# Causal mask moved from TensorE to GpSimd behind the exp, query padding in front, a rebuilt beginning

## The chip, the cores and the metric

The program runs on one core of a Trainium2 chip. The core has five engines with instruction streams of their own: TensorE (PE in the profile, its weight loads PEld), VectorE (DVE), ScalarE (ACT), GpSimd (POOL) and SyncE (SP), which here issues all DMAs. Each engine works through its stream in order. The metric is the device time of one execution in microseconds; three runs of the kernel before gave 1008.39, 1009.94 and 1011.96, a median of 1009.94.

## The reference

Causal attention with a decay bias over 4 batches, 8 heads, 576 positions and head size 64, then two feed-forward layers of 2304 tokens (512 to 2048 to 512).

```python
def _attn_ref(q, k, v, s):
    scores = scale * np.matmul(q, k.transpose(0, 1, 3, 2))
    causal = np.triu(np.ones((S, S), dtype=bool), k=1)
    cum = np.cumsum(np.maximum(s, 0.0), axis=-1)
    bias = -(cum[:, :, :, None] - cum[:, :, None, :])
    scores = np.where(causal, -1000000000.0, scores + np.minimum(bias, 0.0))
    scores = scores - np.max(scores, axis=-1, keepdims=True)
    attn = np.exp(scores)
    attn = attn / (np.sum(attn, axis=-1, keepdims=True) + 1e-09)
    return np.matmul(attn, v)
# x: heads put side by side, [2304, 512]
h = x @ w_in;  x = (h * np.cos(h)) @ w_out
h = x @ w_in2; y = (np.maximum(h, 0) + np.log1p(np.exp(-np.abs(h)))) @ w_out2
```

## The kernel before

**Attention** (`emit_attention`, u = 0 to 31, one head of one batch each). Two heads share one of three slots in the memory that later holds the late weights (`wlate`). A slot has four tiles: `tbk` and `tbq` (K and Q as high and low parts), `tak` and `taq` (high parts on rows 0 to 63, the decay sums and ones on rows 64 and 65, minus ones and the row maxima on rows 96 to 127). One head goes through these steps:

- The row maxima: six matmuls in four PSUM banks (table `MT`), query block by keys, then one DVE reduction per matmul, which adds `mask` and takes the maximum (line 504). DVE joins the two columns of maxima (line 510), TensorE transposes them, ACT copies them out (line 516), and POOL spreads them with an affine select into rows 96 to 127 of `taq` (line 518, `mq` below).
- The scores, keys by queries, in five tiles (table `STL`): `tbk`·`tbq`, then, in each of the five blocks that lie on the diagonal, a bf16 matmul of `ident` and `tri` that adds -1e30 above the diagonal, then `tak`·`taq`, which brings the main product, the decay and minus the maximum.
- ACT takes the exp of a tile into one of four `pf` buffers (line 558); TensorE multiplies it by V (seven matmuls of fp32, each issued as two), ACT evacuates, a DMA stores the head.

Per pair of heads DVE also forms the low parts (lines 486 and 488), and between heads the first eight weight blocks are converted (lines 421 to 429 and 299, 308).

**The beginning.** POOL fills the constant rows of all three slots, one slot after another, and makes `mask`, `ident` and `tri` by selects. DVE computes the decay sums of all 32 heads, and two DMAs bring those of the first pair to rows 64 and 65 of `tak`. Until there is work, TensorE runs small bf16 matmuls on zeros (`warm`, line 376), as many as the planner put there.

**The feed-forward layers** (`emit_moe`) run over token blocks of 512 (one of 256) and 16 blocks of weights, 24 matmuls each; TensorE is in them from about 211 us on.

**What sets the order.** All operations are put into a `Planner`. Each has a due time built from the table `TUNE` (for a head: `max`, `s`, `av` in units of `ud`), and a cost. The planner simulates the engines, lets each take the ready operation with the earliest due time, and writes the instructions in that order; on the chip each engine then follows it in order and waits on semaphores.

Of the kernel before, what the change touches and what calls it, by code (L numbers as in the profile page):

```python
# [22 lines left out]
QS = (0, 256, 576)  # L23
EARLY, SLOT = 8, 4992
GUARD = True
STG = 1.6
TUNE = dict(lam=61.3799, mu=21.9699, sub1=-0.8, sp4=-0.47, ld4=-2.57, load=-3.32, vload=0.9, split=-0.462, max=-0.4135, s=1.63, av=2.34,
            norm=3.5, md=0.14, sd=0.22, ud=5900.0, e=1.2214, o=2.5648, end=3.5, x0=30.0, xd=2364.0, wa=5.755, wb=4.1769,
            wc=1479.6, wd=9828.5, wg=9000.0, pre=9606.0, we=16928.0, wf=6383.3, backlog=1292.7, hz=16175.7)
# [5 lines left out]
BIG = -3.0e38  # L35
ONE_LO = 1.0 - 2.0 ** -24
# [8 lines left out]
class Planner:  # L45
# [49 lines left out]
    def plan(self, penalty=4000.0):  # L95
# [22 lines left out]
        while left:  # L118
            progress = False
            wake = []  # L120
            for e in free:
# [24 lines left out]
                if e == PE and any(k == ("bank", 7) for k, _ in a[0][3].writes):  # L146
                    self.filler = None
# [19 lines left out]
                _, _, i, o = best  # L167
                _, d, fn = o.opts[i]
# [57 lines left out]
def build(tc, qk, v, s, w1, w2, out):  # L226
# [42 lines left out]
    ident = T("ident", [128, 128], BF16)  # L269
    tri = T("tri", [128, 128], BF16)  # L270
# [8 lines left out]
    sraw, cum = heads[0][0:32], heads[2][0:32]  # L279
# [46 lines left out]
    def fill(vt, ap, val, w, engine=POOL):  # L326
# [3 lines left out]
        P.op(vt, [(POOL, 200.0 + n * 0.83, lambda: G.memset(ap, val)) if engine == POOL else (DVE, 70.0 + n * 0.52, lambda: V.memset(ap, val))], (), w)  # L330
# [4 lines left out]
    V.memset(zero, 0.0)  # L335
    V.memset(mask, 0.0)
    V.memset(ident, 1.0)
    V.memset(tri, 0.0)
# [4 lines left out]
    for i in range(3):  # L343
# [3 lines left out]
        slots.append((tbk, tbq, tak, taq))  # L347
    for i in (2, 0, 1):
        tbk, tbq, tak, taq = slots[i]
        vt = -50000.0 + 1000 * (0 if i == 2 else i + 1)  # L350
        ck = [(("c", i), 0)]
        ag = [((("augk", i), h), "z") for h in range(2)]
        fill(vt, tak.bitcast(F32)[64:96, :, 0:S], 0.0, ag)
        fill(vt + 1, tak.bitcast(F32)[:, :, S:], 0.0, ck)
        fill(vt + 1.5, tak.bitcast(F32)[96:128, :, 0:S], -1.0, [(("cm", i), 0)])
        fill(vt + 2, tbk.bitcast(F32)[:, :, S:], 0.0, [(("cb", i), 0)])
        fill(vt + 2, taq.bitcast(F32)[0:96, :, S:], 0.0, [(("cq", i), 0)])
        fill(vt + 3, taq.bitcast(F32)[64:96, :, 0:S], 0.0, [(("augq", i, h), "z") for h in range(2)])
        P.op(vt + 4, [(POOL, 700.0, lambda taq=taq: G.memset(taq.bitcast(F32)[64:66, :, 0:S], 1.0))], r=[(("augq", i, h), "z") for h in range(2)], w=[(("augq", i, h), 0) for h in range(2)])
        if i == 2:  # L360
            P.op(vt + 8, [(POOL, 660.0, lambda: G.affine_select(out=mask, in_=mask, pattern=[[-1, 640]], compare_op=ALU.is_ge, fill=BIG, base=512, channel_multiplier=1))],
                 (), [("mask", 0)])
            P.op(vt + 9, [(POOL, 250.0, lambda: G.affine_select(out=ident, in_=ident, pattern=[[-1, 128]], compare_op=ALU.is_equal, fill=0.0, base=0, channel_multiplier=1))],
                 (), [("ident", 0)])
            P.op(vt + 10, [(POOL, 250.0, lambda: G.affine_select(out=tri, in_=tri, pattern=[[1, 128]], compare_op=ALU.is_ge, fill=-1.0e30, base=0, channel_multiplier=-1))],  # L365
                 (), [("tri", 0)])
            for x in range(3):
                fill(vt + 10, mr[x].bitcast(F32), 0.0, [(("xl", 1, x), "z")])
            fill(vt + 10.1, eye.bitcast(F32), 1.0, [(("xh", 1, 0), "z")])
            P.op(vt + 10.2, [(POOL, 420.0, lambda: G.affine_select(out=eye, in_=eye, pattern=[[-1, 128]], compare_op=ALU.is_equal, fill=0.0, base=0, channel_multiplier=1))],  # L370
                 [(("xh", 1, 0), "z")], [(("xh", 1, 0), 0)])
        fill(vt + 11, vf[:, (i + 1) % 3, 64], 1.0, [(("vo", (i + 1) % 3), 0)])
# [10 lines left out]
    cumh = [cumt[32 * i:32 * i + 32] for i in range(2)]  # L383
    ckeys = [("tbk", 1), ("tbkl", 1)]
# [6 lines left out]
    P.op(vt + 3, [(DVE, dve_t(S, fast=True), lambda: V.tensor_copy(cumh[0], cum))], r=[(nk[1], "cum")], w=[(ckeys[0], "cum")])  # L391
    P.op(vt + 4, sub_hi(cumh[1], cum, cumh[0], S), r=[(nk[1], "cum"), (ckeys[0], "cum")], w=[(ckeys[1], "cum")])
    for i in range(2):
        dma(-41000.0 + i, cdram[:, i], cumh[i].bitcast(F32), r=[(ckeys[i], "cum")], w=[(("cum", i), 0)])
# [395 lines left out]
```

## Time and profile before

| quantity | value |
|---|---|
| median of three runs | 1009.94 us |
| the profiled execution | 1008.23 us |
| its span, first to last instruction | 1006.4 us |
| PE busy | 998.8 us, 99% |
| DVE, ACT, POOL busy | 690.5, 604.0, 51.2 us |
| granted TensorE clock | 1.0 in every slice |

The span and the busy times are of one execution; what lies around the span is 1.8 us. A busy PE includes overlap of consecutive matmuls, so the distance from one start to the next says what a matmul takes. Of the span, the first 23.4 us are the beginning, up to about 224 us runs attention (with the first feed-forward matmuls among it from 211 us), and the rest is the feed-forward layers.

### The profile page before, as it was taken

How to read it: one execution, taken by the hardware profiler on the slowest of the kernel's cores; microseconds unless marked ns; L12 is line 12 of the kernel's file. 1: busy time of each engine (PE TensorE's matmuls, PEld its weight loads, DVE VectorE, ACT ScalarE, POOL GpSimd, SP SyncE). 2: the span in 40 equal slices, each digit the busy share in tenths (PEclk: the TensorE clock that was granted, in tenths of full speed). 3: DMA queues.
4: the chain of work that ended last, by engine and by line, in shares of the span. 5: the costliest groups of instructions: out<-in, count | busy, mean ns of one | idle time of the engine just before them, and what ended most of it. 6: DMA issues, size and time to landing. Idle time of an engine off the chain costs nothing.

```text
span 1006.4 us, 14198 instructions
## 1 busy us (share of the span) xinstructions
PE 998.8 (99%) x5180; PEld 842.3 (84%) x5180; DVE 690.5 (69%) x1284; ACT 604.0 (60%) x1062; POOL 51.2 (5%) x68
## 2 busy tenths in 40 slices
PE   9999999999999999999999999999999999999998
PEld 7888888878888889988888888888888998888886
DVE  8889888879964536445357989995565756555553
ACT  5777777777655445555456668665454655445444
POOL 8111112100000000000000000000000000000000
PEclk9999999999999999999999999999999999999999
DMA  6676666663422212002012335221130201001001
GB/s 209 212 209 188 194 189 185 190 211 113 155 84 91 90 51 101 26 22 64 1 65 99 135 130 189 88 80 49 35 115 1 84 1 42 1 1 42 1 1 42
DMA packets 40488, 95.29 MB, mean 95 GB/s; under 512 B 7074, under 2 KB 13730, under 8 KB 36322
## 3 DMA queue, kind: packets, MB, share of 16 engines
q1 hardware_dynamic: 40418, 94.39, 29.5%
q8 instruction: 40, 0.66, 0.3%
q14 instruction: 30, 0.25, 0.1%
HBM read 66.87 MB, written 18.64 MB: 85 GB/s over the span
## 4 chain that ended last, share of the span: by engine, by line
PE 93%; DVE 2%; DMA 2%; POOL 1%; issue 1%; ACT 0%; SPq 0%; DVEq 0%; POOLq 0%; ACTq 0%
PE bank L322 93%; PE bank L376 1%; DMA stage<-w 1%; DVE bc L504 1%; DMA adram<-num 0%; POOL wlate L330 0%; DMA raw<-rdram 0%; DMA raw<-adram 0%; DVE wlate L488 0%; DVE wlate L486 0%; DVE conv L429 0%; DMA rd<-adram 0%; DVE xl L308 0%; DVE raw L614 0%; POOL tri L365 0%
## 5 line engine op out<-in xcount | busy, mean ns | idle before, releaser
L322 PE MATMUL bank<-xh,wearly 128*128 128x512 f32 (+1 forms) x640 | 193.8, 369 | 1.2 <-DVE pf L658 1.2
L322 PE MATMUL bank<-xh,wlate 128*128 128x512 f32 (+1 forms) x640 | 193.7, 368 | 0.0
L322 PE MATMUL bank<-ghi,wlate 128*128 128x512 f32 (+1 forms) x640 | 193.5, 368 | 0.0
L322 PE MATMUL bank<-ghi,wearly 128*128 128x512 f32 (+1 forms) x640 | 193.5, 368 | 0.0
L299 ACT ACTIVATE ghi<-pf 128x512 fp32r<-128x512 f32 (+1 forms) x160 | 93.8, 587 | 141.9 <-DVE pf L670 92.0
L308 DVE TENSOR_TENSOR glo<-pf,ghi 128x512 fp32r<-128x512 f32 (+1 forms) x160 | 102.0, 637 | 77.4 <-ACT ghi L299 76.9
L322 PE MATMUL bank<-wlate 128*128 128x320 f32 (+9 forms) x576 | 150.5, 363 | 1.3 <-POOL xl L330 1.2
L322 PEld LDWEIGHTS bank<-xh,wearly 128*128 128x128 f32 x640 | 117.3, 189 | 21.7 <-DVE pf L658 1.6
L322 PEld LDWEIGHTS bank<-ghi,wlate 128*128 128x128 f32 x640 | 117.3, 189 | 20.0
L322 PEld LDWEIGHTS bank<-xh,wlate 128*128 128x128 f32 x640 | 117.3, 189 | 19.9
L322 PEld LDWEIGHTS bank<-ghi,wearly 128*128 128x128 f32 x640 | 117.3, 189 | 19.8
L322 PE MATMUL bank<-pf,vf 128*65 128x320 f32 (+4 forms) x448 | 127.9, 384 | 0.0
L322 PE MATMUL bank<-xl,wearly 128*128 128x512 f32 (+1 forms) x320 | 117.9, 369 | 0.0
L322 PE MATMUL bank<-glo,wlate 128*128 128x512 f32 (+1 forms) x320 | 117.9, 368 | 0.0
L322 PE MATMUL bank<-xl,wlate 128*128 128x512 f32 (+1 forms) x320 | 117.8, 368 | 0.0
L322 PE MATMUL bank<-glo,wearly 128*128 128x512 f32 (+1 forms) x320 | 117.8, 368 | 0.0
L322 PEld LDWEIGHTS bank<-wlate 128*128 128x128 f32 (+1 forms) x576 | 95.5, 191 | 17.7 <-POOL xl L330 1.4
L666 DVE SCALAR_TENSOR_TENSOR bc<-pf 128x512 f32<-128x512 f32 (+1 forms) x80 | 51.0, 637 | 81.7 <-ACT pf L664 81.7
L504 DVE CUSTOM_DVE_ANT_0 bc<-bank,mask 128x384 bf16<-128x384 f32 (+3 forms) x192 | 82.0, 468 | 15.7 <-PE bank L322 10.8
L558 ACT ACTIVATE pf<-bank 128x256 f32<-128x256 f32 (+2 forms) x160 | 66.7, 433 | 38.1 <-PE bank L322 33.3
L654 DVE SCALAR_TENSOR_TENSOR pf<-pf,pf 128x512 f32<-128x512 f32 (+1 forms) x80 | 50.7, 635 | 56.3 <-ACT pf L652 56.3
L663 ACT ACTIVATE pf<-bank 128x512 f32<-128x512 f32 (+1 forms) x80 | 44.3, 554 | 68.4 <-PE bank L322 65.7
(75 smaller groups left out, 1331.5 us busy)
## 6 DMA issues: line engine op xcount, KB each, us to landing
stage<-w SPq DMA_DIRECT2D x32, 1024.0 KB
raw<-qk SPq DMA_DIRECT2D x15, 576.0 KB
wlate<-wlate SPq DMA_DIRECT2D x30, 288.0 KB
vf<-v SPq DMA_DIRECT2D x32, 160.0 KB
adram<-num SPq DMA_DIRECT2D x32, 146.2 KB
xdram<-num SPq DMA_DIRECT2D x18, 256.0 KB
out<-num SPq DMA_DIRECT2D x18, 256.0 KB
raw<-adram SPq DMA_DIRECT2D x32, 128.0 KB
```

Of the source, the lines that this page charges most:

```text
L299: opts.append((ACT, act_t(n, psum), (lambda: A.activation(o, i, AF.Copy, scale=1.0 if scale is None else scale))))
L308: return [(DVE, dve_t(n), lambda: V.tensor_tensor(o, a, hi.bitcast(F32), op=ALU.subtract))]
L322: X.matmul(o, a, b, start=st, stop=sp, skip_group_check=skip)
L376: X.matmul(bank[7][:, 0:256], zero[:, 0:128], zero, start=True, stop=True)
L504: P.op(tx + 1, [(DVE, dve_t(w, True) + DX, lambda bk=bk, off=off, w=w, mo=mo, col=col, pr=pr, jk=junk[i if x < 2 else x - 2]: V.tensor_ten ...
L558: P.op(tx + 3, [(ACT, act_t(wt, True) + AX, lambda pt=pt, bk=bk, wt=wt: A.activation(pt[:, :wt], bank[bk][:, :wt], AF.Exp))], r=[(("bank", ...
L654: P.op(te + 2, [(DVE, dve_t(n), lambda a0=a0, a1=a1: V.scalar_tensor_tensor(a1, a1, MAGIC, a0, op0=ALU.subtract, op1=ALU.subtract))], r=[( ...
L663: P.op(te, [(ACT, act_t(n, True), lambda a0=a0, hp=hp: A.activation(a0, hp, AF.Abs))], r=hr, w=[(k0, (tg, "a"))])
L666: P.op(te + 2, [(DVE, dve_t(n), lambda a0=a0, a2=a2: V.scalar_tensor_tensor(a2, a0, 2.0, a0, op0=ALU.subtract, op1=ALU.mult, reverse0=True))],
```

## The change

- **Mask.** The matmuls of `ident` and `tri` go. Behind the exp, a POOL affine select per diagonal block writes zeros above the diagonal of `pf` in place (new line 571), and the matmul with V waits for the last select of its tile. Rows 66 to 95 of `tak` and `taq` (all 0 before) get a staircase in steps of 20 positions, whose product is a very negative score, made by selects from the small tile `cst` (lines 357, 370).
- **Padding.** 64 columns of zeros stand in front of the queries in `taq` (`QP`) and no longer behind, so the query blocks of the maxima end at 64, 192, 320, 448 and 576 instead of 128, 256, 384, 512 and 576. `MT` is cut anew.
- **Beginning.** DVE writes the decay rows of the first pair straight into `tak` (new line 396, `s` comes with the first two heads' rows repeated on other partitions); the fills of POOL wait until the first of them is done (`quiet`), those of slots 0 and 1 for the spread of the maxima of heads 0 and 1 (`later`). The low parts of the first pair are formed in halves. The first weight block and two V tiles are loaded earlier.
- **Order.** `TUNE` and a few costs have other numbers.

```diff
+QP = 640 - S
...
+    quiet = [("cumdone", 0)]
+    P.op(-95000.0, [(POOL, 150.0, lambda: G.affine_select(out=cst[:, 2:4], ...
+        later = ([(("mq", 2, 0), 0)], [(("mq", 2, 1), 1)], [])[i]
+        P.op(vt if later else -94000.0, [(POOL, 1300.0, lambda taq=taq: G.affine_select(out=taq[64:96, :, QP:], in_=cst[64:96, 1:2].unsqueeze(2).broadcast_to((32, 2, S)), pattern=[[0, 2], [1, S]],
+                                                                     compare_op=ALU.is_ge, fill=FAR, base=STEP, channel_multiplier=-STEP))], later, [(("augq", i, h), 0) for h in range(2)])
...
+        fill(vu + 1, tak.bitcast(F32)[:, :, S:], 0.0, [(("c", i), 0)], r=later or quiet)
...
-    P.op(vt + 4, sub_hi(cumh[1], cum, cumh[0], S), r=[(nk[1], "cum"), (ckeys[0], "cum")], w=[(ckeys[1], "cum")])
+    for x in range(2):
+        y = slice(32 + 32 * x, 34 + 32 * x)
+        P.op((vt + 4, -1000.0)[x], [(DVE, dve_t(S), lambda x=x, y=y: V.scalar_tensor_tensor(slots[2][2][64:66, x, 0:S], cumt.bitcast(F32)[y], cst[y, 2 + x:3 + x], cum[y], op0=ALU.mult, op1=ALU.add))],
+             r=[(nk[1], "cum"), (ckeys[0], "cum"), ("cst", 0)], w=[((("augk", 2), x), 0)] + ([("cumdone", 0)] if x == 0 else []))
...
-    MT = [[(4, 0, 320, 4, 0), (0, 0, 128, 0, 320)], [(1, 0, 256, 1, 0), (4, 320, 256, 9, 256)], [(2, 0, 384, 2, 0)], [(3, 0, 512, 3, 0)]]
+    MT = [[(4, 0, 320, 4, 0), (1, 0, 192, 1, 320)], [(3, 0, 448, 3, 0), (0, 0, 64, 0, 448)], [(2, 0, 320, 2, 0)], [(4, 320, 256, 9, 0)]]
...
-                    dma(t + 20 + x, tak.bitcast(F32)[64:66, x, 0:S], cumt.bitcast(F32)[x:x + 33:32], r=[(i, "cum") for i in ckeys], w=[((kaugk, x), 0)])
...
-                if x != 1:
-                    ml.append((o[:, 0:min(w, 128)], ident, tri[:, :min(w, 128)], False, False, True, 0))
-                ml.append((o, tak[:, sl, ks], taq[:, sl, qs:qs + w], False, True, True, w))
+                ml.append((o, tak[:, sl, ks], taq[:, sl, QP + qs:QP + qs + w], False, True, True, w))
...
+            done = bt
+            for i, (j, qs, off, w) in enumerate(lst):
+                if qs == 128 * j:
+                    dw = min(w, 128)
+                    P.op(tx + 4 + i, [(POOL, 220.0 + 1.4 * dw, lambda z=pt[:, off:off + dw], dw=dw: G.affine_select(
+                        out=z, in_=z, pattern=[[1, dw]], compare_op=ALU.is_ge, fill=0.0, base=0, channel_multiplier=-1))],
+                        r=[(("pf", pi), done)], w=[(("pf", pi), (bt, i))])
+                    done = (bt, i)
```

In TensorE's stream, in the middle of attention, a stretch of the kernel before reads as follows (`wlate` is score and maximum matmuls, `pf,vf` the matmuls with V, each of which is two instructions).

```order
L322 MATMUL bank_68<-wlate 128x320
L322 LDWEIGHTS ident
L322 MATMUL bank_68<-tri,ident 128x128
L322 MATMUL bank_70<-pf_95,vf 65x320
L322 MATMUL bank_68<-wlate 128x320
L322 MATMUL bank_69<-wlate 128x192
L322 LDWEIGHTS ident
L322 MATMUL bank_69<-tri,ident 128x128
```

A stretch of the changed kernel at the same stage:

```order
L323 MATMUL bank_70<-pf_96,vf 65x64
L323 MATMUL bank_72<-pf_94,vf 65x320
L323 MATMUL bank_68<-wlate 128x320 x2
L323 MATMUL bank_66<-wlate 128x256 x2
L323 MATMUL bank_69<-wlate 128x192 x2
L323 MATMUL bank_69<-wlate 128x64 x2
L323 MATMUL bank_71<-pf_95,vf 65x128
```

The two score matmuls of a block now stand side by side, and no mask stands among them.

POOL's stream at the beginning, before (`xl` are the maxima's scratch tiles, L518 the first two spreads of maxima):

```order
L363 AFFINE_SELECT ident<-ident 128x128
L365 AFFINE_SELECT tri<-tri 128x128
L330 MEMSET xl_84 128x128 x3
L330 MEMSET xh_82 128x128
L370 AFFINE_SELECT xh_82<-xh_82 128x128
L330 MEMSET vf 128x5
L330 MEMSET wlate 32x2x576
L330 MEMSET wlate 128x2x64
...
L359 MEMSET wlate 2x2x576
L330 MEMSET vf 128x5
L518 AFFINE_SELECT wlate<-xl_84 32x640
L518 AFFINE_SELECT wlate<-xh_82 32x640
```

And in the changed kernel (L357 and L370 make the staircase rows, L527 is the spread of maxima, L571 the new mask):

```order
L357 AFFINE_SELECT wlate<-cst 32x2x576
L370 AFFINE_SELECT wlate<-cst 32x2x576
L363 AFFINE_SELECT mask<-mask 128x640
L331 MEMSET wlate 128x2x64 x2
...
L370 AFFINE_SELECT wlate<-cst 32x2x576
L527 AFFINE_SELECT wlate<-xl_84 32x640
L357 AFFINE_SELECT wlate<-cst 32x2x576
L331 MEMSET wlate 96x2x64
L571 AFFINE_SELECT pf_94<-pf_94 128x128
L527 AFFINE_SELECT wlate<-xh_82 32x640
```

The first spread stands ahead of the fills of two slots instead of behind them, and from there on masks and spreads share one queue.

DVE's stream from the decay sums to the first reductions (L504, L513), before:

```order
L391 CAST wlate<-num 32x576
L308 TENSOR_TENSOR wlate<-num,wlate 32x576
L486 TENSOR_TENSOR wlate<-raw_85,wlate 64x2x576
L488 SCALAR_TENSOR_TENSOR wlate<-raw_85,wlate 64x1152
L504 ISA bc,mx<-bank_66,mask 128x256
```

And in the changed kernel:

```order
L393 CAST wlate<-num 96x576
L396 SCALAR_TENSOR_TENSOR wlate<-wlate,cst,num 2x576
L309 TENSOR_TENSOR wlate<-num,wlate 32x576
L396 SCALAR_TENSOR_TENSOR wlate<-wlate,cst,num 2x576
L513 ISA bc,mx<-bank_65,mask 128x320
```

The low parts of the first pair moved from ahead of the first reductions to behind them, in halves of 576 columns, and two small operations joined the chain.

## Rows read from the trace of the kernel before

**Rows 1.** The page, busy time, share and instructions of each engine.

```profile
PE 998.8 (99%) x5180; PEld 842.3 (84%) x5180; DVE 690.5 (69%) x1284; ACT 604.0 (60%) x1062; POOL 51.2 (5%) x68
```

**Rows 2.** Stretches: length, PE, PEld, DVE, ACT, POOL busy (count), clock, DMA share, GB/s.

```profile
0.00:23.41 23.41, 20.95 (x158) 17.04 (x158) 20.66 (x55) 12.13 (x15) 21.51 (x38) 1.00 0.63 194
23.41:224.50 201.09, 199.73 (x1232) 165.33 (x1230) 174.72 (x483) 149.28 (x310) 29.65 (x31) 1.00 0.67 198
224.50:1002.60 778.10, 778.08 (x3792) 659.97 (x3792) 495.16 (x747) 441.98 (x737) 0.00 (x0) 1.00 0.19 64
```

**Rows 3.** The chain that ended last, first 60 us: shares by engine and line.

```profile
by line: PE bank L322 69.0%; PE bank L376 15.1%; POOL wlate L330 6.6%; issue 2.4%; POOL tri L365 2.3%; POOL mask L361 1.4%; POOL ident L363 1.3%; POOL xl L330 0.7%; POOL wlate L359 0.2%; POOLq L361 0.1%; POOLq L365 0.0%; POOLq L783 0.0%
```

**Rows 4.** Timeline of PE around 134 us: start, us, what.

```profile
132.92 0.23 PE L322 MATMUL bank<-tri,ident 128*128 128x128 bf16 x1
132.99 0.74 PE L322 MATMUL bank<-pf,vf 128*65 128x320 f32 x2
133.33 0.64 PE L322 MATMUL bank<-wlate 128*128 128x320 f32 x2
...
134.29 0.20 PE L322 MATMUL bank<-tri,ident 128*128 128x64 bf16 x1
134.33 0.77 PE L322 MATMUL bank<-pf,vf 128*65 128x320 f32 x2
134.70 0.55 PE L322 MATMUL bank<-wlate 66*128 66x320 f32 x1
```

**Rows 5.** Timeline of PE at 184 us, with no mask in front.

```profile
184.18 0.71 PE L322 MATMUL bank<-pf,vf 128*65 128x320 f32 x2
184.48 0.52 PE L322 MATMUL bank<-wlate 66*128 66x256 f32 x1
```

**Rows 6.** Groups by form on PE, the mask: busy us, mean ns.

```profile
L322 PE MATMUL bank<-tri,ident 128*128 128x128 bf16 x128 | 29.3, 230 | 0.0
L322 PE MATMUL bank<-tri,ident 128*128 128x64 bf16 x32 | 6.6, 206 | 0.0
```

**Rows 7.** Groups by form on DVE, widest and narrowest reduction of the maxima.

```profile
L504 DVE CUSTOM_DVE_ANT_0 bc<-bank,mask 128x512 bf16<-128x512 f32 x32 | 21.8, 681 | 0.5
L504 DVE CUSTOM_DVE_ANT_0 bc<-bank,mask 128x128 bf16<-128x128 f32 x32 | 8.9, 277 | 0.0
```

**Rows 8.** Timeline of PE in the beginning, the warm-up matmuls (the second row is part of the first).

```profile
1.18 7.16 PE L376 MATMUL bank<-num 128*128 128x256 bf16 x43 [1.18 <-DVE num L335]
...
5.64 2.71 PE L376 MATMUL bank<-num 128*128 128x256 bf16 x22
9.51 1.15 PE L322 MATMUL bank<-wlate 66*128 66x320 f32 x6 [1.16 <-POOL xl L330]
```

**Rows 9.** Timeline of DVE in the beginning.

```profile
2.76 0.78 DVE L388 TENSOR_SCALAR num<-num 32x576 f32<-32x576 f32 x1 [1.07 <-DMA num<-s]
...
4.95 1.41 DVE L391 CAST wlate<-num 32x576 fp32r<-32x576 f32 x1
...
7.57 1.35 DVE L486 TENSOR_TENSOR wlate<-raw,wlate 64x1152 fp32r<-64x1152 f32 x1
...
10.34 0.42 DVE L504 CUSTOM_DVE_ANT_0 bc<-bank,mask 128x256 bf16<-128x256 f32 x1
...
21.46 1.64 DVE L486 TENSOR_TENSOR wlate<-raw,wlate 64x1152 fp32r<-64x1152 f32 x1
```

**Rows 10.** Timeline of POOL, the first two spreads of maxima.

```profile
21.15 0.75 POOL L518 TENSOR_SCALAR_AFFINE_SELECT wlate<-xl 32x640 fp32r<-32x640 f32 x1
21.85 1.86 POOL L518 TENSOR_SCALAR_AFFINE_SELECT wlate<-xh 32x640 fp32r<-32x640 f32 x1
```

**Rows 11.** Groups by form on ACT and POOL: busy us, mean ns.

```profile
L558 ACT ACTIVATE pf<-bank 128x320 f32<-128x320 f32 x64 | 27.8, 434 | 11.0 <-PE bank L322 10.2
...
L518 POOL TENSOR_SCALAR_AFFINE_SELECT wlate<-xl 32x640 fp32r<-32x640 f32 x16 | 16.2, 1012 | 84.6 <-ACT xl L516 84.5
...
L330 POOL MEMSET xl<- 128x128 f32 x3 | 0.5, 205 | 0.0
```

More of the change, by code (lines that the diff above doesn't have):

```diff
@@ L35 @@
 BIG = -3.0e38
+STEP, FAR = 20, -1.2676506002282294e30
 ONE_LO = 1.0 - 2.0 ** -24
@@ L167, in plan @@
                 _, _, i, o = best
+                if e == PE and any(k == ("bank", 7) for k, _ in o.writes):
+                    self.filler = None
                 _, d, fn = o.opts[i]
@@ L324, in mms, with fill @@
         return [(PE, d, go)]
-    def fill(vt, ap, val, w, engine=POOL):
+    def fill(vt, ap, val, w, engine=POOL, r=()):
         n = 1
@@ L329, in fill @@
             n *= x
-        P.op(vt, [(POOL, 200.0 + n * 0.83, lambda: G.memset(ap, val)) if engine == POOL else (DVE, 70.0 + n * 0.52, lambda: V.memset(ap, val))], (), w)
+        P.op(vt, [(POOL, 80.0 + n * 0.88, lambda: G.memset(ap, val)) if engine == POOL else (DVE, 70.0 + n * 0.52, lambda: V.memset(ap, val))], r, w)
     for i in range(2):
@@ L347, in build @@
         slots.append((tbk, tbq, tak, taq))
+    quiet = [("cumdone", 0)]
+    P.op(-95000.0, [(POOL, 150.0, lambda: G.affine_select(out=cst[:, 2:4], in_=cst[:, 2:4], pattern=[[32, 2]], compare_op=ALU.is_ge, fill=-1.0, base=32, channel_multiplier=-1))], (), [("cst", 0)])
     for i in (2, 0, 1):
         tbk, tbq, tak, taq = slots[i]
[L350 to L359, printed above, removed]
@@ L360, in build @@
-        if i == 2:
[L361 to L366, printed above, removed]
+        vt = (700.0, 20000.0, -50000.0)[i]
@@ new lines, in build @@
+        fill(vt + 0.1 if later else -93000.0, taq.bitcast(F32)[0:96, :, 0:QP], 0.0, [(("cq", i), 0)], POOL if later else DVE, later)
+        fill(vu + 1, tak.bitcast(F32)[:, :, S:], 0.0, [(("c", i), 0)], r=later or quiet)
+        fill(vu + 2, tbk.bitcast(F32)[:, :, S:], 0.0, [(("cb", i), 0)], r=later or quiet)
+        if i == 2:
+            P.op(-50001.0, [(POOL, 760.0, lambda: G.affine_select(out=mask, in_=mask, pattern=[[-1, 640]], compare_op=ALU.is_ge, fill=BIG, base=512, channel_multiplier=1))],
+                 quiet, [("mask", 0)])
@@ L371, in build @@
+            P.op(vt + 3.2, [(POOL, 380.0, lambda: G.affine_select(out=eye, in_=eye, pattern=[[-1, 128]], compare_op=ALU.is_equal, fill=0.0, base=0, channel_multiplier=1))],
                  [(("xh", 1, 0), "z")], [(("xh", 1, 0), 0)])
-        fill(vt + 11, vf[:, (i + 1) % 3, 64], 1.0, [(("vo", (i + 1) % 3), 0)])
+        P.op((-40000.0, 19900.0, -91000.0)[i], [(POOL, 1300.0, lambda tak=tak: G.affine_select(out=tak[64:96, :, 0:S], in_=cst[64:96, 0:1].unsqueeze(2).broadcast_to((32, 2, S)), pattern=[[0, 2], [1, S]],
+                                                                     compare_op=ALU.is_ge, fill=0.0, base=STEP, channel_multiplier=-STEP))], (quiet, later, [])[i], [((("augk", i), h), "z") for h in range(2)])
@@ L382, in build @@
     cumt = slots[1][0].rearrange("p h n -> p (h n)")[:, 0:S]
-    cumh = [cumt[32 * i:32 * i + 32] for i in range(2)]
-    ckeys = [("tbk", 1), ("tbkl", 1)]
+    cuml = slots[1][1].rearrange("p h n -> p (h n)")[:, 0:S]
+    cumh = [cumt[0:32], cuml[0:32]]
+    ckeys = [("tbk", 1), (("tbql", 1), 0)]
     vt = -60000.0
```

75 lines of the change are left out of this document (40 added, 35 removed).

## The prediction

> **What bounds the kernel now.** I read the page's busy times first, then the stretches, then the chain of waits at the beginning, then TensorE's timeline in the middle of attention, and last the groups by form of the operations that the change touches. TensorE is busy 998.8 of 1006.4 us [rows 1], and the stretches show where it is not: it loses most before 23.4 us; from there to 224.5 us it is busy 199.7 of 201.1 us, and in the feed-forward layers 778.1 of 778.1 [rows 2]. So an instruction less on TensorE shortens the run by what it occupies, as long as no other engine comes up beside it. The nearest is VectorE, busy 174.7 us in the attention stretch, 87% [rows 2]; GpSimd has 29.7 us of work there. In the beginning the chain runs over the warm-up matmuls (line 376): 15.1% of the first 60 us, 9.0 us, all behind the first real matmul at 9.51 us [rows 3, 8]. These only pass the time; they and what lies ahead of 9.51 us are lost time, some 19 us in all.
>
> **The mask matmuls.** 128 of 128 columns and 32 of 64 go [rows 6]. Their mean times of 230 and 206 ns contain the overlap, so I take starts. A mask of 128 starts at 132.92 and the next matmul at 132.99: 0.07 us; a 128-column stream of 0.44 ns a column (below) is 0.06, so I take 0.065. The matmul with V behind it then takes 0.34 us to the next other start (132.99 to 133.33) [rows 4], the same one behind a long matmul 0.30 (184.18 to 184.48) [rows 5]: the load of V has only the short mask to hide under, and 0.04 us of it show. That is 0.105 us each, 13.4 us for 128. A mask of 64 occupies 0.04 us (134.29 to 134.33), and the V matmul behind it 0.37 (134.33 to 134.70) [rows 4]; but what it will follow instead is a 64-column score matmul, just as short, so the 0.07 stay and I count 32 x 0.04 = 1.3 us. Sum 14.7 us. Bounds: 9.6 if the exposed load shows again somewhere else in all cases (128 x 0.065 + 1.3), 17.6 if all 160 give 0.11.
>
> **The padding.** The six maximum matmuls of a head have 1856 columns now (320, 128, 256, 256, 384, 512) and 1600 afterwards (320, 192, 448, 64, 320, 256). The feed-forward stretch has 3840 matmuls less a few that run earlier, with 1.77 million columns, in 778.1 us [rows 2]: 0.44 ns a column. 256 columns are 0.113 us, 3.6 us for 32 heads. Against it the narrowest is now 64 instead of 128 wide and hides 0.03 us less of the load behind it (0.07 against 0.04 above): 1.0 us. I take 2.6 us, bounds 1.6 and 3.6. VectorE gains too: between 512 and 128 columns its reduction goes from 681 to 277 ns [rows 7], 1.05 ns a column, so 0.27 us a head, 8.6 us of its 174.7.
>
> **The beginning.** The first real matmul starts at 9.51 us, behind 43 warm-up matmuls, of which 21 had started before 5.64 us [rows 8], and behind the decay rows, which a DMA brings after the operation that follows the cast. The changed order has 24 warm-ups first, done by about 6 us, and no DMA: the sums arrive at 2.76 us, maximum and scan end at 4.95 [rows 9], the cast takes 1.41 us beside a running fill and perhaps 0.5 without one (GpSimd's fills now wait), and the new operation of 576 columns about 0.7, half of the 1.35 us of a 1152-column one [rows 9]. That is 6.2 to 7.1 us; the transfer of `s` is three times as large and may add 0.3. I take 6.5 us, 3.0 us earlier. After it the changed order has 71 warm-ups where 81 stood, at 0.111 us (9.0 us by 81) 1.1 us less. Against the sum of 4.1 us stands VectorE: it did the low parts of the first pair (from 7.57 us) while it had nothing else, before the first reduction at 10.34 [rows 9]; now these 2.7 us come between the reductions of heads 0 and 1, and two new operations stand in front. The first spread of maxima, at 21.15 us [rows 10] behind the fills of two slots, can start soon after its maxima are there, some 6 us earlier; but heads 2 and 3 are paced by VectorE, which is no further by then. I take 3.0 us in all, bounds a loss of 1 (VectorE gives all of it back) and a gain of 5.
>
> **What is added.** 160 selects on GpSimd, between exp and the matmul with V. No row has one in this place. For its price the bounds are 0.205 us, a fill of the same 128x128 that reads nothing, and 0.75 us, the undisturbed select of 640 columns [rows 10, 11]; with a fifth of the columns it is nearest to the fill, and I take 0.25. That is 40 us of GpSimd's time in the stretch on top of 29.7, so GpSimd does not become full. Whether TensorE waits is a matter of distance. Priced by the rows above, the matmuls between the last score matmul of a tile and its first V matmul were worth at least 0.7 us and in the middle 1.5 to 2.1 (by kind of tile), and with an exp of 0.43 us [rows 11] and its handovers that was enough, since TensorE hardly waited [rows 2]. In the changed order they are worth at least 1.2 and in the middle 2.2 to 3.6 us. The select and one handover more, about 0.5 us, thus fit in the added distance. What can break it is a select that is held up. The spread at 21.85 us took 1.86 us instead of 0.75, beside a subtraction that took 1.64 instead of 1.35 [rows 9, 10], and the mean of these selects is 1.01 [rows 11]. A hold of about 1 us on a part of the tiles is more than the shortest distances bear. Queued behind a held select are the other masks and the spread of the next head's maxima, for which its score matmuls wait. Bounds: 0 if the distance bears all, 42 us if TensorE waits the mean excess of 0.26 us (1.01 less 0.75) on each of 160 tiles. I take 3 us: 0.26 us on about 12 of the 160, since half of the tiles have a distance of more than twice what they need.
>
> The held spread bears on a rule of the Trainium skill, page "SBUF — State Buffer", section "Who interferes with whom": a GpSimd instruction that reads SBUF and a VectorE instruction with two SBUF inputs (or in a two-port mode) shut each other out for the whole instruction, while one that only writes is free of the two-input kind. The subtraction and the spread above agree with it. By that rule the fill is too cheap a neighbour for the new selects, and the change puts 160 readers beside an engine that is 87% busy; taken to its end this is the first rival below.
>
> Sum against the profiled execution: 1008.23 - 14.7 - 2.6 - 3.0 + 3 = 990.9 us. That execution is 1.7 us below the median of the runs shown, so for a median I forecast 992 us. The other renumbered due times move feed-forward work only within a stretch where TensorE has no gap, and I cost them at nothing; what hides them is that VectorE and ScalarE have 495 and 442 us of work in 778 [rows 2]. Were that cover gone, TensorE would wait at the change of stage, and I would double the 1.4 us that it is idle in the whole attention stretch [rows 2].
>
> **The rivals.**
> - VectorE becomes the bound of attention. For: 87% busy, and selects and its two-input operations shut each other out. Its work falls to 174.7 - 8.6 = 166.1 us, while TensorE's falls to 199.7 - 17.3 = 182.4. If each select takes its 0.205 us from VectorE, that is 166.1 + 32.8 = 198.9, and the stretch stays where it is: only the beginning's 3 us and 0.8 us are left, 1006 us. Against: where a hold shows in the rows, it is beside a subtraction of a pair, of which attention has 32, and not beside the 192 reductions.
> - TensorE waits for held masks, and it becomes slower. Place: the matmul with V of the diagonal tiles, behind the select in GpSimd's queue. The gain without waits is 20.3 us, and it decides from 0.127 us a tile, half of the mean excess of 0.26 us. At three quarters (31 us) the time is 1021 us. For: a mean of 1.01 us against 0.75, and four `pf` buffers, which now stay taken for longer. Against: the distance in the order has grown by more than an undisturbed select needs.
> - No waits, and the beginning gives its 5 us: 1009.94 - 17.3 - 5 = 987.6, or 985 with the higher bound for the masks.
>
> **How the numbers follow.** Forecast 0.74, with its own range of 985 to 999 from the bounds of masks and beginning and up to 9 us of waits; the case without waits 0.07; VectorE as the bound 0.10; held masks 0.09. A measurement of this kernel can tell about 0.3%, 3 us, from no change. Faster: 0.74 + 0.07 and half of the 0.10, 0.86; within 0.3% the other half, 0.05; slower 0.09. The range of 983 to 1004 leaves out 0.19 above (and next to nothing below).
>
> **What would show it.** In the profile of the changed kernel: attention's PE busy time near 182 us with the first feed-forward matmuls about 17 us earlier; the first real matmul near 6.5 us; the first spread near 15 us; 128x128 selects near 0.25 us in the middle and some over 1 us beside subtractions; idle time of PE in front of V matmuls of about 3 us. The forecast is wrong if VectorE is over 95% busy between 25 and 200 us, or if PE's idle time there is over 10 us and is put down to POOL, or if the matmuls with V stay at 0.34 us without the masks.

## The result and the profile after

| | before | after |
|---|---|---|
| median of the runs | 1010.45 us (1008.39 to 1011.96) | 997.36 us (995.03 to 1000.12) |
| ratio | | 0.9873, interval 0.9841 to 0.9905 |
| the profiled execution | 1008.23 us | 998.2 us |

The changed kernel is 12.8 us (3.2 either way) faster; the forecast was 992, with a range of 983 to 1004. The time is within the range and 5 us above the forecast. Below, the difference of two kernels is the difference of their ratios to the kernel before, times 1010 us, since each was timed beside its own runs of it.

The page's busy times of the changed kernel, which answer to [rows 1]:

```profile
PE 982.8 (99%) x4991; PEld 835.1 (84%) x4991; DVE 684.2 (69%) x1289; ACT 605.6 (61%) x1063; POOL 124.2 (12%) x223
```

The stretches of the changed kernel (length, then busy time of PE, PEld, DVE, ACT and POOL with counts, granted clock, DMA share, GB/s), against [rows 2]:

```profile
0.00:24.00 24.00, 20.58 (x139) 16.50 (x140) 20.52 (x60) 13.07 (x19) 15.64 (x33) 1.00 0.64 210
24.00:208.00 184.00, 179.61 (x1045) 155.87 (x1044) 164.54 (x477) 143.61 (x302) 108.57 (x191) 1.00 0.72 207
208.00:992.00 784.00, 782.04 (x3810) 662.65 (x3809) 499.14 (x754) 447.85 (x743) 0.00 (x0) 1.00 0.20 65
```

PE lost 16.0 us of busy time, but its idle time grew. It is 4.4 us between 24 and 208 us now, and 2.0 us behind 208 us, at the change of stage. In [rows 2] the attention stretch of before has 1.4 us, but 1.2 of these are its own wait at the change of stage, which the cut at 224.50 us puts into that stretch. Up to 205 us it was idle for only 0.2 us (a stretch and PE's timeline of the kernel before):

```profile
23.41:205.00 181.59, 181.40 (x1138) 150.48 (x1137) 158.16 (x461) 134.59 (x284) 29.65 (x31) 1.00 0.67 196
```

```profile
224.52 0.50 PE L322 MATMUL bank<-xh,wearly 128*128 128x512 f32 x1 [1.19 <-DVE pf L658]
```

GpSimd works 109 us in attention instead of 30, and VectorE is still at 89%.

The beginning of VectorE, timeline of the changed kernel (start, us, engine, line, operation), against [rows 9]:

```profile
3.71 0.46 DVE L390 TENSOR_SCALAR num<-num 96x576 f32<-96x576 f32 x1 [1.84 <-DMA num<-s]
4.20 1.75 DVE L391 TENSOR_TENSOR_SCAN num<-num 96x576 f32<-96x576 f32 x1
5.99 0.46 DVE L393 CAST wlate<-num 96x576 fp32r<-96x576 f32 x1
6.56 0.81 DVE L396 SCALAR_TENSOR_TENSOR wlate<-wlate,cst,num 2x576 fp32r<-2x576 f32 x1
...
9.80 0.49 DVE L513 CUSTOM_DVE_ANT_0 bc<-bank,mask 128x320 bf16<-128x320 f32 x1
```

And of TensorE, its first real matmul, against [rows 8]:

```profile
7.52 0.98 PE L323 MATMUL bank<-wlate 66*128 66x320 f32 x6 [1.21 <-ACT wlate L476]
```

The sums arrive at 3.71 us, 0.95 later than before. The first matmul is 2.0 us earlier, the first reduction only 0.54. The view names ScalarE's copy of line 476, which ended at 7.52 us, as what released the matmul; the decay rows ended at 7.37 (6.56 and 0.81), so which of the two held it isn't settled.

TensorE in the middle of attention, timeline of the changed kernel, against [rows 4, 5]:

```profile
135.15 0.65 PE L323 MATMUL bank<-wlate 128*128 128x320 f32 x2
135.63 0.70 PE L323 MATMUL bank<-pf,vf 128*65 128x320 f32 x2
135.93 0.89 PE L323 MATMUL bank<-wlate 128*128 128x256 f32 x5
...
148.19 0.28 PE L323 MATMUL bank<-wlate 128*128 128x64 f32 x1
148.30 0.79 PE L323 MATMUL bank<-pf,vf 128*65 128x320 f32 x2
148.68 0.84 PE L323 MATMUL bank<-wlate 128*128 128x320 f32 x3
```

Behind a long score matmul the matmul with V takes 0.30 us (135.63 to 135.93), behind one of 64 columns 0.38, as it did behind a mask.

The selects: groups by form on POOL (busy us, mean ns), and who waits for them between 24 and 208 us (us in all, times, longest):

```profile
L571 POOL TENSOR_SCALAR_AFFINE_SELECT pf<-pf 128x128 f32<-128x128 f32 x128 | 61.5, 486 | 47.0 <-ACT pf L565 45.1
L571 POOL TENSOR_SCALAR_AFFINE_SELECT pf<-pf 128x64 f32<-128x64 f32 x32 | 12.6, 395 | 0.1
```

```profile
PEld bank L323 <- POOL pf L571: 4.2, 8, 0.9
PE bank L323 <- POOL pf L571: 1.9, 5, 0.6
```

The median of all 160 is 292 ns, the longest 1504. Of the 45 that took over 0.45 us, 41 ran beside a VectorE operation with two operands in SBUF, of the 111 under 0.31 us 36. TensorE's weight load waits eight times for a select, and its matmul five times.

The change of stage, PE's timeline of the changed kernel:

```profile
213.36 0.39 PE L323 MATMUL bank<-ghi,wearly 128*128 128x512 f32 x1
215.70 0.50 PE L323 MATMUL bank<-glo,wearly 128*128 128x512 f32 x1 [1.96 <-DVE glo L309]
```

VectorE stood 2.03 us in its queue before a multiply whose operand a DMA brought (line 629, at 214.24 us), with the operation that TensorE needed behind it.

### The profile page after: what moved, and what is told of

The parts are those of the page before. It is cut to its first block, busy times and chain, and to the rows that moved or that the text cites. A ratio compares the mean times of both kernels' runs of the same rounds, so it can differ in the third digit from the quotient of the medians.

```text
span 996.2 us, 14023 instructions
## 1 busy us (share of the span) xinstructions
PE 982.8 (99%) x4991; PEld 835.1 (84%) x4991; DVE 684.2 (69%) x1289; ACT 605.6 (61%) x1063; POOL 124.2 (12%) x223
## 4 chain that ended last, share of the span: by engine, by line
PE 90%; DVE 3%; DMA 2%; ACT 1%; POOL 1%; issue 1%; SPq 0%; DVEq 0%; POOLq 0%; ACTq 0%
PE bank L323 90%; DMA wlate<-wlate 1%; POOL pf L571 1%; DVE bc L513 1%; DMA raw<-adram 1%; ACT pf L565 1%; DMA raw<-rdram 0%; DVE wlate L495 0%; DVE raw L629 0%; DVE wlate L497 0%; DMA num<-s 0%; POOL wlate L527 0%; ACT wlate L482 0%; DVE wlate L396 0%; DMA adram<-num 0%
## 5 line engine op out<-in xcount | busy, mean ns | idle before, releaser
L323 PE MATMUL bank<-xh,wlate 128*128 128x512 f32 (+1 forms) x640 | 206.6, 368 | 0.0
L323 PE MATMUL bank<-ghi,wlate 128*128 128x512 f32 (+1 forms) x640 | 205.9, 368 | 0.0
L323 PE MATMUL bank<-ghi,wearly 128*128 128x512 f32 (+1 forms) x640 | 205.2, 368 | 0.0
L323 PE MATMUL bank<-xh,wearly 128*128 128x512 f32 (+1 forms) x640 | 205.1, 369 | 0.0
L323 PE MATMUL bank<-wlate 128*128 128x320 f32 (+9 forms) x576 | 134.4, 344 | 4.2 <-DMA wlate<-wlate 1.8
L323 PE MATMUL bank<-pf,vf 128*65 128x320 f32 (+4 forms) x448 | 125.5, 383 | 2.0 <-POOL pf L571 1.9
L323 PEld LDWEIGHTS bank<-wlate 128*128 128x128 f32 (+1 forms) x576 | 93.0, 190 | 20.1 <-DVE conv L430 1.6
L513 DVE CUSTOM_DVE_ANT_0 bc<-bank,mask 128x320 bf16<-128x320 f32 (+3 forms) x192 | 75.6, 430 | 7.8 <-PE bank L323 4.0
```

The source lines that it names most:

```text
L513: P.op(tx + 1, [(DVE, dve_t(w, True) + DX, lambda bk=bk, off=off, w=w, mo=mo, col=col, pr=pr, jk=junk[i if x < 2 else x - 2]: V.tensor_ten ...
```

## The experiments

**No selects.** The order is the changed kernel's, the place of the selects in it too.

```diff
-    P.op(tx + 4 + i, [(POOL, 220.0 + 1.4 * dw, lambda ...: G.affine_select(out=z, ...))],
+    P.op(tx + 4 + i, [(POOL, 220.0 + 1.4 * dw, lambda: None)],
```

> The changed kernel with the 160 mask selects planned but not issued, so every other engine keeps its order; the block above the diagonal is masked only by the staircase of 20 positions. It gives what the selects cost in waits and in disturbance of VectorE. Theory A (waits behind the selects ate the shortfall of 5 us against the forecast): 5 to 8 us faster than the changed kernel, about 990 to 992. Rival B (the selects are hidden, the beginning or transfers ate it): within 2 us of the changed kernel, about 996.

Measured: 994.61 us, ratio 0.9845 (0.9824 to 0.9866), 2.8 us below the changed kernel, between the two expectations; the two intervals overlap. In the two profiles the same matmuls stand in the same order, and up to 205 us the distances from start to start are in sum 5.3 us longer with selects. This profile also showed a thing that varies from run to run. Its timeline of PE at the change of stage, and stretches around it:

```profile
211.35 0.80 PE L323 MATMUL bank<-glo,wearly 128*128 128x512 f32 x1 [2.88 <-DVE glo L309]
```

```profile
205.00:210.00 5.00, 3.48 (x16) 2.55 (x14) 1.68 (x4) 2.52 (x4) 0.00 (x0) 1.00 0.79 242
210.00:215.00 5.00, 3.65 (x9) 2.88 (x10) 5.00 (x10) 3.04 (x5) 0.00 (x0) 0.55 0.24 50
215.00:220.00 5.00, 5.00 (x19) 4.04 (x18) 5.00 (x6) 3.80 (x6) 0.00 (x0) 0.77 0.47 107
```

TensorE was idle for 2.88 us, and then had a granted clock of 0.55, near its lower level of 1.2 GHz. The lead of 5.3 us over the changed kernel's profile was 1.9 at the end of the span (994.3 against 996.2); the longer wait makes 0.9 of the difference, and the fall of the clock, by what is left, about 2.5. In the changed kernel no fall followed the wait of 1.96 us.

**The kernel before without its mask matmuls.** The order is that of before; the decay is clipped on the other side, so that exp sees no large numbers.

```diff
-            for o, a, b, st, sp, skip, _ in lst:
+            for o, a, b, st, sp, skip, n in lst:
+                if n == 0:
+                    continue
-    V.tensor_scalar_max(sraw, sraw, 0.0)
+    V.tensor_scalar_min(sraw, sraw, 0.0)
```

> The kernel before with its 160 mask matmuls planned but not issued, order kept; the mask is left out, and the decay is clipped to its negative part (minimum for maximum) so that the exps stay finite. It gives the gross price of the mask on TensorE. The forecast's row price (0.105 us for 128, 0.04 for 64 columns): 14.7 us faster than before, about 995.5. Rival (only their streams count, the exposed load shows again elsewhere): 9.6 us, about 1001.

Measured: 1005.41 us, ratio 0.9955 (0.9939 to 0.9971): 4.5 us, a third of what I had priced. The profile is of an execution of 1009.08 us, 3.7 above the median, so it shows more loss than the median has. Its stretch of attention, and waits there (us in all, times, longest):

```profile
23.41:224.50 201.09, 195.80 (x1083) 166.02 (x1081) 175.69 (x485) 149.65 (x313) 32.48 (x31) 0.98 0.68 200
```

```profile
DVE bc L506 <- PE bank L324: 8.6, 8, 1.8
PEld bank L324 <- DVE xl L512: 6.7, 12, 2.3
...
PEld bank L324 <- DVE mx L506: 5.0, 13, 0.7
...
DVE rd L587 <- DMA rd<-adram: 4.2, 2, 2.7
...
PE bank L324 <- DVE xl L512: 3.2, 7, 1.8
...
PE bank L324 <- DVE mx L506: 0.9, 3, 0.3
```

Instruction by instruction against the kernel before, the distances across the missing masks are 7.6 us shorter up to 205 us, and the other distances 6.9 us longer. Of the 6.9 us, 4.5 lie between 127 and 137 us, at one wait and what followed it (below). TensorE waits for VectorE's maxima (lines 506, 512), 25 times in its weight loads and ten times, 4.1 us, in its matmuls, and VectorE for TensorE's banks. I read this as two engines that keep an order made for matmuls that are no longer there; the trace doesn't show that reason by itself. The largest single wait, on VectorE and then on PE:

```profile
127.70 0.18 DVE L587 TENSOR_SCALAR rd<-rd 128x18 f32<-128x18 f32 x1 [2.72 <-DMA rd<-adram]
...
128.77 0.17 DVE L512 TENSOR_TENSOR xl<-mx 128x5 fp32r<-128x5 f32 x1
```

```profile
128.99 0.48 PE L324 MATMUL bank<-xh,xl 128*128 128x128 f32 x1 [1.82 <-DVE xl L512]
```

A small step of the normalization (line 587) waits for its transfer and holds the reductions behind it. In the next stretch the granted clock was 0.50, which is the level of 1.2 GHz:

```profile
130.00:135.00 5.00, 5.00 (x19) 4.02 (x18) 4.06 (x14) 2.67 (x6) 0.65 (x1) 0.50 0.38 91
```

**The mask back on TensorE, everything else as changed, order planned anew.**

```diff
+                if x != 1:
+                    ml.append((o[:, 0:min(w, 128)], ident, tri[:, :min(w, 128)], False, False, True, 0))
...
-                if qs == 128 * j:
+                if False:
```

> The changed kernel with the mask back on TensorE (identity and triangle matmuls, planned anew) and no selects; padding, beginning and due times stay. It gives what moving the mask is worth net of waits. If the move is most of the change (forecast 14.7 less 3): 10 to 12 us slower than the changed kernel, about 1008. Rival (the due times of the new order alone gave most): within 5 us of the changed kernel.

Measured: 1013.53 us, ratio 1.0023 (1.0003 to 1.0043): 15.2 us above the changed kernel and even slower than before. TensorE was idle for 6.0 us between 24 and 208 us of its profile, and between 215 and 240 us the clock was 0.86, so its size isn't the masks' alone. It also shows that the new numbers, the padding and the beginning don't make the kernel faster by themselves while the planner has masks to place. That led to a repeat in a fixed order (below).

**No V loads behind the third head** (V of other heads is used).

```diff
-        dma(at(st["vload"]) ..., vl[:, 0:64], v[u], ...)
+        dma(at(st["vload"]) ..., vl[:, 0:64], v[u], ..., skip=u > 2)
```

> The changed kernel without the V loads of heads 3 to 31 (those heads use old V tiles), order kept: 4.6 MB less in the attention stage, about 14% of its traffic. Rival C (transfers limit the attention stage, whose DMA share is 0.72 to 0.76): 4 us or more faster. Theory A (only waits behind selects matter): within 2 us of the changed kernel.

Measured: 994.78 us, ratio 0.9854 (0.9835 to 0.9872), 1.9 us below the changed kernel, with intervals that overlap. The share of the transfers in the time is small, and not settled by this run.

**The padding alone, in the kernel before.**

```diff
+QP = 640 - S
-    MT = [[(4, 0, 320, 4, 0), (0, 0, 128, 0, 320)], [(1, 0, 256, 1, 0), (4, 320, 256, 9, 256)], [(2, 0, 384, 2, 0)], [(3, 0, 512, 3, 0)]]
+    MT = [[(4, 0, 320, 4, 0), (1, 0, 192, 1, 320)], [(3, 0, 448, 3, 0), (0, 0, 64, 0, 448)], [(2, 0, 320, 2, 0)], [(4, 320, 256, 9, 0)]]
```

> The kernel before with the padding and the new cut of the maximum matmuls alone, planned anew with its own due times. The forecast's term (TensorE columns): 2.6 us faster than before, about 1007. Rival D (padding helps through VectorE's shorter reductions only where VectorE holds TensorE up, which it did not do before): within 1 us of the term, not more than 4 us either.

Measured: 1007.74 us, ratio 0.9977 (0.9968 to 0.9987): 2.3 us less, 1.3 to 3.2.

**The same, with the mask matmuls not issued and the decay clipped** (both edits above).

> The same with the mask matmuls planned but not issued (mask left out, decay clipped to its negative part), order kept. Theory D (without the masks VectorE's reductions held TensorE up, as the wait for them of 9.4 us in the trace without masks says, and the padding takes 0.27 us a head off them): 5 us or more below the pad-only kernel, 999 to 1002. Rival (the masks are worth only 4.4 us in any order): 1003.

Measured: 1005.72 us, ratio 0.9953 (0.9935 to 0.9970): 2.4 us below the padding alone. Across the missing masks 7.8 us are gained up to 205 us, and elsewhere 2.8 lost, 2.0 of them at one wait of 1.6 us (its clock was 0.53 in the 3.5 us behind it). Neither expectation has this time. With VectorE's work made shorter by the padding the old order still doesn't give what the masks were to bring.

**The x multiply of the second block later in the plan**, so that it stands less far ahead of its transfer.

```diff
-   emit_x(which, k, lambda kc, c0=c0: cb[max(c0 - 8, 0)] + kc * TUNE["xd"])
+   emit_x(which, k, lambda kc, c0=c0: cb[max(c0 - (5 if which == 0 and k == 1 else 8), 0)] + kc * TUNE["xd"])
```

> The changed kernel with the preparation of the second token block due three weight blocks later, so that VectorE does not wait for its transfer ahead of the first output matmul (TensorE stood 1.96 us there at 213 us). Theory E (that wait, and in some runs a fall of the clock after it, is part of the shortfall): 2 to 4 us faster than the changed kernel, and its runs lie closer together. Rival: no difference, since the same transfers are late elsewhere.

Measured: 994.85 us, ratio 0.9855 (0.9837 to 0.9874): 1.8 us below the changed kernel, with intervals that overlap. The wait of 2 us at the change of stage became three of 0.3 to 0.5 us in its profile. Of the versions that leave nothing out it has the lowest median, but it isn't told apart from the changed kernel.

**The same, with the steps of the normalization 4500 units of due time later** (lines 600 and 601 and their store).

```diff
-  P.op(tn + 2, [(DVE, 160.0, ...
-  P.op(tn + 3, [(DVE, 200.0, ...
+  P.op(tn + 4502, [(DVE, 160.0, ...
+  P.op(tn + 4503, [(DVE, 200.0, ...
```

> The same, and the two VectorE steps of the normalisation (and the store behind them) due 4.5 us later, so that VectorE does not stand in front of their transfer (4.0 us in three places). Theory E: another 1 to 2 us, about 992 in all. Rival: nothing, since VectorE's waits there are hidden by the distance of two heads.

Measured: 996.36 us, ratio 0.9864 (0.9849 to 0.9879): no gain beside the one before. Its profile had a clock of 0.76 and 0.89 between 210 and 220 us, which that of the one before hadn't.

**The mask matmuls in the changed kernel's own order.** No selects; the masks ride with the second score matmul of a tile, and nothing else moves. TensorE's other 4991 matmuls stand in the same order as in the kernel without selects.

```diff
+        def both():
+            X.matmul(o[:, 0:min(w, 128)], ident, tri[:, :min(w, 128)], start=False, stop=False, skip_group_check=True)
+            go()
...
-                    P.op(tx + i + 0.1 * y, mms(ml), r=rr + old + end, ...)
+                    P.op(tx + i + 0.1 * y, masked(ml, o, w) if y and x != 1 else mms(ml), r=rr + old + end, ...)
```

> The changed kernel with its selects not issued (their place in the order kept, so the triangle is not masked by them) and the 160 mask matmuls issued again, each just ahead of the second score matmul of its tile, in the changed kernel's own order; nothing else stands elsewhere. Theory A (the forecast's step): a mask matmul costs the step that its rows show, 0.105 us, so 15 us above the kernel without selects (994.6): 1009 to 1010. Theory B: what it costs is the difference of the same step with and without it, 0.07 us between a score and a V matmul and 0.04 between two score matmuls, 0.049 in the mean: 8 us above, 1002 to 1003. Under B the rest of what the change gained comes from the order that is planned without them.

Measured: 1008.84 us, ratio 0.9983 (0.9971 to 0.9995): 13.9 us (2.4 either way) above the kernel without selects. Theory A, the forecast's step, is right for this order, and theory B wrong. PE's timeline with the masks (they appear as `num` of line 333), and the same matmuls in the kernel without selects:

```profile
135.59 0.50 PE L325 MATMUL bank<-wlate 128*128 128x320 f32 x1
135.93 0.23 PE L333 MATMUL bank<-num 128*128 128x128 bf16 x1
135.97 0.39 PE L325 MATMUL bank<-wlate 128*128 128x320 f32 x1
136.20 0.70 PE L325 MATMUL bank<-pf,vf 128*65 128x320 f32 x2
```

```profile
127.31 0.65 PE L323 MATMUL bank<-wlate 128*128 128x320 f32 x2
127.79 0.70 PE L323 MATMUL bank<-pf,vf 128*65 128x320 f32 x2
```

0.61 us against 0.48. The mask occupies 0.04 (135.93 to 135.97), and the matmul behind it takes 0.08 longer. Summed up to 205 us, the distances across the masks are 11.0 us longer and the others 3.0. With the matmul behind it, a mask is worth 0.11 us in the mean here; counted in the same way it is 0.07 in the order of before. Theory B had left out the matmul behind. And nothing waits any more:

```profile
24.00:215.00 191.00, 191.00 (x1192) 160.67 (x1191) 162.17 (x476) 145.44 (x300) 35.70 (x34) 1.00 0.69 196
```

PE is busy for all of the 191 us. So this order hides every other engine while TensorE carries the masks, and still has room when they go. The order of before did not, at least in the execution that was profiled: up to 205 us it went from 0.2 us of idle time to 4.6 without them, 1.8 of these in the one wait shown.

**The changed kernel with the number table of before.**

```diff
-TUNE = dict(lam=60.337, mu=30.3528, sub1=-0.8, sp4=-0.5165, ..., hz=30743.0)
+TUNE = dict(lam=61.3799, mu=21.9699, sub1=-0.8, sp4=-0.47, ..., hz=16175.7)
```

> The changed kernel planned with the number table (due times, costs, weights) of the kernel before. Theory P (part of the gain lies in the new numbers): 1 to 6 us slower than the changed kernel's 997.4, 999 to 1003, with more waits over 0.3 us ahead of TensorE's matmuls in attention. Theory Q (the numbers matter little, what counts is that the masks are out of TensorE's plan): within 1.5 us of it, 996 to 999.

Measured: 1003.56 us, ratio 0.9938 (0.9915 to 0.9960): 6.6 us (4.0 either way) slower than the changed kernel. Theory P holds; the middle is even a little above its range. TensorE's matmuls wait ten times for selects between 24 and 208 us, 5.3 us in all, where the changed kernel has five times and 1.9 us; waits over 0.3 us of any kind are seven against six, so the sign that theory P named hardly shows. One place costs most, here on DVE, POOL and PE in turn:

```profile
29.08 1.35 DVE L495 TENSOR_TENSOR wlate<-raw,wlate 64x1152 fp32r<-64x1152 f32 x1
30.47 0.17 DVE L519 TENSOR_TENSOR xl<-mx 128x5 fp32r<-128x5 f32 x1
30.67 1.38 DVE L497 SCALAR_TENSOR_TENSOR wlate<-raw,wlate 64x1152 fp32r<-64x1152 f32 x1
32.08 1.23 DVE L433 SCALAR_TENSOR_TENSOR conv<-stage,conv 128x1024 uint32<-128x1024 uint32 x1
```

```profile
29.40 4.05 POOL L571 TENSOR_SCALAR_AFFINE_SELECT pf<-pf 128x128 f32<-128x128 f32 x4 [0.98 <-ACT pf L565]
33.53 1.78 POOL L527 TENSOR_SCALAR_AFFINE_SELECT wlate<-xh 32x640 fp32r<-32x640 f32 x1
```

```profile
33.51 1.34 PE L323 MATMUL bank<-pf,vf 128*65 128x320 f32 x2 [1.87 <-POOL pf L571]
```

```profile
33.00:36.00 3.00, 2.49 (x7) 1.45 (x8) 1.66 (x2) 0.80 (x2) 2.53 (x3) 0.50 0.89 246
```

Four selects take 4.05 us, while VectorE has three long operations with two operands in SBUF (lines 495, 497 and 433) nearly without a pause; one takes 0.29 us undisturbed. TensorE waits 1.87 us behind them, its granted clock is 0.50 in the next 3 us, and the next spread of maxima, held as well, is late for the next head. This is the rival of held masks, in one place. How much of the 6.6 us is such falls of the clock isn't shown: the mean clock of these six executions is 0.995 to 0.998, that of the changed kernel's four 0.997 to 1.0.

**No selects, and the x multiply later.** Both edits above.

> The later place for the x multiply of the second attention block, as in the run that was timed with it (994.9), and no selects issued (their place in the order kept; the triangle is left unmasked). If the selects cost 3 us whatever happens at the change of stage, 991.5 to 992.5. If the 994.6 of the kernel without selects was held up by the fall of the granted clock after TensorE's 3 us of idle time there, and that wait is gone here, 988 to 991. If the later place gains nothing beside it, 994 to 995.

Measured: 992.73 us, ratio 0.9820 (0.9803 to 0.9838): 3.5 us (2.6 either way) below the kernel with the later multiply, and 2.5 below the one without selects. The first expectation has the number nearest to it; the larger recovery of the second did not come.

**The x multiply later, and q and k of the second pair ahead of the first V and weight loads.**

```diff
-    dma(at(f - STG) if which or f else -35000.0, sg, w[f].bitcast(U32), ...)
+    dma(at(f - STG) if which or f else -34300.0, sg, w[f].bitcast(U32), ...)
-    dma(at(st["vload"]) if u > 1 else -35100.0 + u, vl[:, 0:64], v[u], ...)
+    dma(at(st["vload"]) if u > 1 else -34320.0 + u, vl[:, 0:64], v[u], ...)
```

> The later place for that x multiply, and the q and k of the second pair of heads loaded ahead of the first V and weight loads instead of behind them. If TensorE's wait of 1.3 us near 32 us for the transfer into that slot is what the beginning lost of its gain: 993 to 994 against 994.9, with head 3's transpose near 30 instead of 32 us. If the V and weight loads that now come later take its place as the late transfer: 995 to 997.

Measured: 999.50 us, ratio 0.9886 (0.9868 to 0.9904), 3.1 us (2.6 either way) slower than without this edit. The wait of 1.15 us for the transfer, which the changed kernel has at 32.00 us, is gone, and in its place PE waits for the spreads and the selects on GpSimd:

```profile
30.37 0.54 PE L323 MATMUL bank<-wlate 128*128 128x256 f32 x2 [0.88 <-POOL wlate L527]
32.11 0.76 PE L323 MATMUL bank<-pf,vf 128*65 128x192 f32 x4 [0.56 <-POOL pf L571]
```

So the wait did move, but to GpSimd and not to another transfer; neither expectation had that.

## Why the prediction came out as it did

By the runs the way from before to after goes in three parts: padding, beginning and order with the masks still there, -1.7 us (1.2 either way); the masks taken out, -13.9 (2.4); the selects, +2.8 (3.9). Together -12.8. The forecast had -5.6, -14.7 and +3.0. The split holds for this sequence of steps; with the masks taken out first, in the old order, they give 4.5.

- *The masks, "0.105 us each", in sum 14.7.* The size holds, 13.9, and the step too: 0.11 us with the matmul behind it, though split otherwise (0.07 and 0.04 us). It isn't a property of the instruction. In the order of before the step is worth 0.07 us, and the removal gave 4.5 us there and 2.4 in that order with the padding. I read from [rows 2] that an instruction less on TensorE shortens the run "as long as no other engine comes up beside it", and took VectorE's 87% as room. It was the mean over a stretch in which the two engines wait for each other in a fixed order. In the traces of the two runs in the old order most of what was lost lies at one wait for VectorE and the fall of the clock behind it, and the rest in short waits; how it divides in a median execution is open. The rival with VectorE as the bound gave 1006 us, and the old order without masks took 1005.4, but that is a coincidence: the rival's mechanism is selects that take VectorE's time, and that run has none. That the changed kernel doesn't lose its masks' gain in this way is a matter of its order; which of the order's new numbers does it isn't shown.
- *"The other renumbered due times", costed "at nothing".* This step failed. They were read as feed-forward work only; the table also sets the due times of attention. With the table of before the rest of the change gives 6.3 us in place of 12.8 (ratio 0.9938). The reason given for the nothing was misread as well. That TensorE has "no gap" behind 224.50 us comes of where the stretch was cut, right behind its wait of 1.2 us at the change of stage, and this wait is most of the 1.4 us that the prediction gives to attention.
- *The padding, 2.6.* Alone it gave 2.3, within 1.3 to 3.2.
- *The beginning, 3.0.* The -1.7 us above contain the padding's 2.3, so beginning and order together gave nothing with the masks still there (+0.6, with 1.5 either way). Of the 4.5 us between the forecast gain of 17.3 and the measured 12.8, 3.9 lie here. In the trace the first matmul came 2.0 us earlier instead of 3.0: the cast (0.46 us) and the new operation (0.81) took what I had estimated (0.5 and 0.7), but `s` arrived 0.95 us later, where I had 0.3, and the scan took 1.75. The step "GpSimd's fills now wait" was wrong in the trace: the select of `mask` starts at 3.80 us and runs beside the scan, well before the decay rows at 6.56 on which it depends in the plan. That wait exists only there. The cast was short all the same, with a select (from 5.70 us) and a fill (from 6.10) beside it, so a fill beside it isn't by itself what made it 1.41 us before. Then 1.15 us of the gain go at 32.00 us to a transfer into the slot of the second pair, which I had not seen; taking it away by an earlier load made things slower.
- *The first spread near 15 us.* It starts at 14.82.
- *The selects, +3.* The runs give 2.8 (3.9 either way) and 3.5 (2.6 either way). Median 0.29 us against my 0.25, but the mean is 0.47, so they take 74 us of GpSimd's time where I had 40. Weight loads wait eight times and matmuls five, where I said about 12. PE's idle time in attention is 4.4 us instead of 0.2; 1.9 of it is waits for selects (I had 3) and 1.8 waits for transfers, for which I had no term.
- *The matmuls with V, 0.34 us behind a mask.* Behind long score matmuls they take 0.30 now, as read from [rows 5].
- *The change of stage.* TensorE's idle time there is 2.0 us instead of 1.2, from a multiply that waits for its transfer; I had named such a wait as what comes when the cover is gone. Placing it later gave 1.8 us (with selects) and 2.5 us (without), each with an interval that reaches to nothing.
- *First feed-forward matmul 17 us earlier.* It came at 211.07 us and now at 199.73, 11.3 earlier, in an execution whose whole gain is 10.0 us; the longer wait at the change of stage takes 0.8 of the rest back.

The Trainium skill, page "SBUF — State Buffer", section "SBUF: two separate sides", says that a GpSimd instruction that reads SBUF and a VectorE instruction with two SBUF inputs exclude each other for the whole instruction. The four selects of 4.05 us agree with it: the three held ones end 0.10 to 0.16 us behind the ends of the VectorE operations beside them. That it did not become the bound of attention I put down to how few such pairs the order has side by side; no run here tests that.

Left open: why some executions of one and the same kernel differ by 5 us (995.03 to 1000.12). Places at which the granted clock fell after some 2 to 3 us without TensorE work differ between the profiles, and two of the four executions had a mean clock of 0.997 and 0.998, but those of 995.03 and 998.2 us both had 1.0. Open too is what the new numbers would give in the kernel before, which was not run.

## What to carry to other kernels

The price of an instruction on the busiest engine is found by putting it in or taking it out in the order that will run; in an order that was planned with it, its removal can turn into waits of in-order engines for each other, and here two thirds of the price didn't come. When a change renumbers a planner, run its code with the old numbers: that is one experiment, and here half of the gain went with the new ones. An engine at 87% over a stretch is not by itself room; look for who waits for whom in short pieces. And look where a stretch is cut before calling it free of gaps.

## What the runs showed of the hardware

- After TensorE had nothing to do for 2.88 us (no selects), 1.87 (table of before) and 1.82 us (no masks in the old order) its granted clock was 0.55, 0.50 and 0.50 in the next 3 to 5 us. In the changed kernel 1.96 us were followed by 1.00. I had not reckoned with a cost behind a wait; in the first case it was about 2.5 us. Waits of this length didn't tell by themselves whether the clock would fall.
- A bf16 mask matmul of 128 columns occupies 0.04 us between two score matmuls, and the matmul behind it mostly takes 0.06 to 0.08 us longer. When the mask comes right behind a matmul with V (31 of the 160), the distance across it grows by 0.11 to 0.27 us, and the next one is up to 0.16 us shorter.
- A select of 128x128 takes 0.29 us in the median, and up to 1.50 beside VectorE's operations with two operands in SBUF.
